# Attention keys turned in blocks of 128, expert numbers cast on VectorE, and a new order for all but the first stage

## The chip, the cores and the metric

The kernel runs on one core of a Trainium2 chip. The metric is the device time of one execution in microseconds. Before the change the median of three runs is 1021.76 us (1020.55 to 1022.34).

## What is computed

Three layers follow one another. Their inputs and outputs are float32.

```python
# 1. local attention: B=4, H=8, S=768, D=64; chunks of 32 queries
for c in range(nc):
    l_start, r_end = max(0, 32*c - 16), min(S, 32*c + 32 + 8)
    k_full = concat([mem_k, k[:, :, l_start:r_end]])        # 8 memory keys + up to 56 keys
    a = softmax(scale * q_c @ k_full.T)                     # with 1e-9 in the sum
    out[:, :, chunk c] = a @ concat([mem_v, v[:, :, l_start:r_end]])
# 2. MLP over 3072 tokens of 512: w_in 512 x 2048, w_out 2048 x 512 (float64 words)
h = x @ w_in;  x = (h * tanh(softplus(h))) @ w_out
# 3. routed MLP: each token goes to one of 8 experts (512 -> 1024 -> 512)
expert_idx = argmax(cosine(x, expert_emb) / tau);  gate = softmax(...)[expert_idx]
out[mask_e] = gate * (relu(x[mask_e] @ w1[e]) @ w2[e])
```

Products that need more than one pass of TensorE's reduced float32 are taken as three: high part by high part, high by low, low by high.

## The kernel before

**Attention.** The work is cut into 24 pairs P, each two blocks of 64 queries; six pairs make one batch. A pair loads its queries (`q`) and its keys in two pieces: `k1`, 8 memory rows and 96 keys (104 rows), and `k2` (72 rows). TensorE turns them (`Tq`, `Tk` 0, `Tk` 1, all on L511) into `p_qT`, `p_kT` and `p_k`. ScalarE or VectorE then copies from these into `kT`, a tile with four groups of 64 columns, one per chunk of 32 queries: 8 memory keys, 24 keys before, 32 of the chunk (three copies from `p_kT`, two from `p_k`, L334). Then come the scores `S` (L559), maximum, exponential, normalization, the transposition `PT` (L602) and the product with the values `V` (L621), whose result is split into `xt`.

**MLP.** Eight blocks of 384 tokens by 16 feature chunks give 128 steps. Step s has `mm_h` (12 matmuls of 384 columns, L732), a chain of about ten element operations on ScalarE and VectorE (L736 to L761), and `mm_y` (9 matmuls of 512 columns, L778). The attention of later blocks runs between the MLP steps of earlier ones.

**Routing and experts.** Tokens are routed in two groups: the first 21 tiles of 128 tokens (group 1) and all (group 2). In a group, VectorE works out positions and counts, TensorE counts (`cnt`, L1060) and builds the table of tokens per slot (`tab`, L1218, copied off by L1230); `ef` holds the expert number of each unit as float32, `ei` the same as integers (L1175). There are 16 units u: 0 to 2 from group 1, the rest from group 2. A unit is a pair of slots (256 tokens) or a single (128). It gathers its tokens (GpSimd, L1288, into `vn`), turns them (`xT`, L1331), splits them (`xs`, L1334 and L1348), loads 8 pieces of expert weights of 512 KB (`eraw`, L1314, address from `ei`, read by L1302; whether it differs from the expert before from `ci`, L1304), splits these in `ehi` (L334) and `elo` (L1367), and multiplies: four `H` (L1395; L1429 for singles) and four to eight `Y` (L1485). The result is scattered by GpSimd (L1511).

**What sets the order.** All steps are jobs of the class `Plan`. `order` is a list scheduler: from the jobs whose predecessors are planned it takes the one of lowest rank among those that can start soonest, with assumed durations (`on=`). The rank is the job's place in the program plus a number from the table `NUDGE`, by kind of job and stage. The outcome is one fixed sequence for each engine, which works through it in order. Waits between engines are semaphores. Loads are issued from SyncE's queue (SP), gathers and scatters from GpSimd's.

Of the kernel before, what the change touches and what calls it, by code (L numbers as in the profile page):

```python
# [86 lines left out]
def between(a, b):  # L87
# [12 lines left out]


NUDGE = dict(
    acta0=-0.6, acta1=-1.74, acta2=50.36, actb0=-1.76, actb1=-96.54, actb2=-81.79, actb3=-42.59, att00=40.88,
    att01=6.03, att02=-14.41, att03=12.63, att04=-3.12, att05=6.33, att06=-6.99, att07=-18.03, att10=10.46, att11=7.93,
    att12=-2.03, att13=-0.28, att14=-5.39, att15=28.34, att16=0.19, att17=-11.65, att20=7.04, att21=-2.49, att22=6.84,
    att23=0.68, att25=11.02, att26=-13.24, att27=2.06, att30=-0.41, att31=-70.31, att32=-0.58, att33=-1.39,
    att35=-0.38, att36=-1.67, att37=-67.52, att40=0.45, att41=-0.43, att42=13.06, att43=-2.17, att44=-38.4,
    att45=12.86, att46=9, att47=-2.37, att50=-1.08, att51=-18.11, att52=-6.46, att53=252.42, att54=-0.22, att55=-3.21,
    att56=-1.09, att57=2.56, att60=-5.29, att61=2.16, att63=-69, att64=-3.49, att65=145.06, att66=-0.33, att67=-14.14,
    att70=-0.37, att71=-329.92, att72=0.25, att73=-193.55, att74=-10.54, att75=-2.18, att76=-1.27, e00=-1.37, e01=8.52,  # L110
    e10=3.1, e11=23.17, e20=-86.99, e21=1, e30=0.07, e31=1.64, e40=10.43, e41=28.57, e50=1.56, e51=-2.1, e60=-22.39,
    e61=17.86, e70=-0.44, e71=-5.41, em=3.37, en0=24.71, en1=-0.52, en2=4.38, en3=27.95, en4=-27.14, en5=-7.94,
    hh0=0.33, hh1=-9.8, hh2=7.9, ld00=-15.25, ld01=24.83, ld10=34.53, ld11=33.12, load0=8.15, load1=17.34, load10=5.31,
    load2=-45.54, load3=-3.15, load4=-2.18, load5=-0.64, load7=3.07, load9=4.58, mm_y0=20.47, mm_y1=14.69, mm_y2=275.2,
    mm_y3=-0.5, out0False=-95.98, out0True=2.61, out1False=4.84, out2False=6.58, raw0=-8.26, raw1=5.15, raw10=24.34,
    raw11=134.61, raw2=-9.44, raw3=-3.37, raw4=-0.07, raw5=-13.38, raw6=29.5, raw7=26.79, raw9=-0.21, route=3.96,
    rows0=21.85, rows1=0.04, rows2=2.04, split0=0.59, split10=130.91, split11=-16.93, split3=-2.85, split4=-6.67,
    split5=17.18, split6=34, split9=27.54, xs0=0.9, xs1=0.33, xs2=-187.61, ye0=0.64, ye1=82.2, ye2=137.26, ye3=-2.03,
    ye4=8.94, ye5=-5.92, yre0=-32.64, yre1=-4.26, yre3=-2.85, yre4=22.58, yre5=-10.72,
)  # L120
ATT = dict(q=0, k1=0, k2=0, Tq=1, Tk=1, qT=1, kT=1, v=2, mem=2, mem0=2, S=3, mx=3, ex=4, rg=5, rc=5, norm=5, PT=6, pT=6, V=7, xh=7, xl=7)

# [42 lines left out]
class Plan:  # L165
# [115 lines left out]
def attn_moe_moe_kernel(ctx, tc, q, k, v, mem_k, mem_v, w_in, w_out, emb, tau, w1, w2, cst, out, ydbg=None):  # L281
# [143 lines left out]
    def pairs(P):  # L425
# [39 lines left out]
        def load_k1(e):  # L465
            if not spare:
                if P == 0:
                    tl["k"] = att.tile([128, H, D], F32, tag="kn", bufs=1, name="kn")
                tl["kn", P] = tl["k"]
            t = tl["kn", P]  # L470
            if spare or i == 0:
                dma(e, t[0:NMEM], mem_k[b].rearrange("h p d -> p h d"))
            get_keys(e, t, NMEM, w, w + K1 - NMEM)

        def load_k2(e):
            t = tl["kn2", P] = wp.tile([K2, H, D], F32, tag=k2t, name="kn2") if first else tl["k"]
# [30 lines left out]
        def turn(name, src, rows):  # L507
            def f(e):
                p, c = psa([128, J, rows], "p_" + name), tl[src, P]
                for n in range(J):  # L510
                    nc.tensor.transpose(p[:, n, :], c[0:rows, 2 * n:2 * n + 2, :].rearrange("p h d -> p (h d)"), ident[:rows, :rows])  # L511
                tl["T", name, P] = p
                if name == "qT":
                    tl["qT", P] = own(qts, [128, J, 2 * QB], "qT", bufs=1)
                if name == "kT":
                    tl["kT", P] = own(ktt, [128, J, 4, SEEN], "kT", bufs=1)
            return f

# [117 lines left out]
        plan.dma(("q", P), load_q, size=rows(128), rank=L(0), after=[("issue", "k2", P - 1)] if P else [], get=[(qkt[0], qs)], **iss(1))  # L639
        plan.dma(("k1", P), load_k1, size=rows(K1), rank=L(0.1), after=[("issue", "q", P)] if P > 1 else [("issue", "k1", 0)] if P else [], get=[] if spare else [("kn", ks)], use=[qs] if spare else [], **iss(3 if i == 0 else 2 if spare else 1, A if P < 2 else "SP"))  # L640
        plan.dma(("k2", P), load_k2, size=rows(K2), rank=L(0.2), after=[("issue", "q" if P < 2 else "k1", P)], get=[(k2t, k2s)], **iss(2 if i == NQB - 2 else 1))
        kh = qs if spare else ks
        vh = [("vn", P, h) for h in range(2)]
        for h in range(2):
# [7 lines left out]
        qh, kt, xb = ("qT", P), ("kT", P), [("X", P, a) for a in range(2)]  # L652
# [275 lines left out]
    def routing():  # L928
# [51 lines left out]
        def group(g):  # L980
# [286 lines left out]
    def unit(u, base, x, cols, main=True, after=0, then=0):  # L1267
# [379 lines left out]
```

## Time and profile before

| | |
|---|---|
| median of 3 runs | 1021.76 us |
| the profiled execution, its own time | 1021.15 us |
| its span, first to last instruction | 1019.4 us |
| mean granted TensorE clock | 0.991 |
| TensorE busy / VectorE busy / ScalarE busy / GpSimd busy | 991.5 / 809.0 / 648.8 / 189.5 us |
| the chain that ended last | TensorE 76%, VectorE 8%, DMA 7%, issue 5% |

The profile is of one execution. TensorE is busy for 97% of the span, in an unbroken stretch from about 110 to 660 us (attention and MLP) and with some gaps behind (routing and experts). The first 110 us load and split the MLP's weights. Row groups below name engines PE (TensorE), DVE (VectorE), ACT (ScalarE), POOL (GpSimd) and SP (SyncE, `SPq` its queue).

### The profile page before, as it was taken

The page shows a single profiled execution, that of the slowest core. Times are in us where ns is not written, and L with a number is a line of the kernel's source. Part 1 is how long each engine was busy: PE and PEld are TensorE (multiplying, and loading weights), DVE is VectorE, ACT ScalarE, POOL GpSimd, SP SyncE. Part 2 cuts the span into 40 slices and gives each one's busy share as a digit, 9 for nine tenths or more (in the row PEclk, how much of TensorE's full clock was granted, in tenths as well). Part 3 has the DMA queues.
Part 4 walks back from the last instruction along what each step waited for, and adds up shares of the span by engine and source line. Part 5 has one row for each costly group of instructions (what it writes and reads, how often), then busy time and mean ns, then how long its engine had stood idle before and what let it go on. Part 6 is the DMA issues. An engine that isn't in the chain of part 4 may idle for free.

```text
span 1019.4 us, 22817 instructions
## 1 busy us (share of the span) xinstructions
PE 991.5 (97%) x8575; PEld 879.2 (86%) x8575; DVE 809.0 (79%) x1799; ACT 648.8 (64%) x1534; POOL 189.5 (19%) x142
## 2 busy tenths in 40 slices
PE   7899999999999999999999999999989999999997
PEld 6678888898888888888888899888979988988986
DVE  4889999669899869769869867979948667777972
ACT  4788888776877777778777767757424334443431
POOL 5000100000000000000000000011136455555742
PEclk9989999999999999999999999999989999999999
DMA  9997661233645234325313100089089868467300
GB/s 181 253 237 200 168 184 45 59 128 97 184 132 135 74 78 134 84 46 145 84 25 122 30 20 20 1 272 327 32 279 371 280 229 296 150 218 246 127 29 23
DMA packets 171817, 146.36 MB, mean 144 GB/s; under 512 B 105114, under 2 KB 134410, under 8 KB 171444
## 3 DMA queue, kind: packets, MB, share of 16 engines
q1 hardware_dynamic: 164868, 128.53, 43.5%
q0 software_dynamic: 5104, 15.89, 4.6%
q8 instruction: 69, 1.13, 0.5%
q10 hardware_dynamic: 1728, 0.43, 0.3%
q14 instruction: 48, 0.39, 0.1%
HBM read 137.11 MB, written 16.53 MB: 151 GB/s over the span
## 4 chain that ended last, share of the span: by engine, by line
PE 76%; DVE 8%; DMA 7%; issue 5%; POOL 2%; SPq 1%; ACT 0%; POOLq 0%; DVEq 0%
PE p_h L732 23%; PE p_y L778 23%; PE p_y L1485 10%; PE p_h L1395 9%; DMA eraw<-in_moe_w_dram 2%; PE p_h L1429 2%; DMA kn<-in_k_dram 2%; PE p_X L621 2%; PE p_S L559 2%; POOL elo L1367 1%; SPq L319 1%; PE p_PT L602 1%; PE p_xT L1331 1%; PE p_qT L511 1%; DMA qn<-in_q_dram 1%
## 5 line engine op out<-in xcount | busy, mean ns | idle before, releaser
L732 PE MATMUL p_h<-xt,win_h 128*128 128x384 f32 x1024 | 268.9, 344 | 0.6 <-DVE rn L761 0.5
L732 PEld LDWEIGHTS p_h<-xt,win_h 128*128 128x128 f32 x1024 | 185.3, 191 | 10.2 <-DVE rn L761 1.8
L732 PE MATMUL p_h<-xt,win_l 128*128 128x384 f32 x512 | 173.9, 340 | 0.0
L334 ACT CAST ehi<-eraw 128x1024 fp32r<-128x1024 f32 x89 | 92.9, 1049 | 120.0 <-PE p_y L1485 67.7
L778 PE MATMUL p_y<-wout_h,gh 128*128 128x512 f32 x384 | 157.1, 409 | 0.0
L778 PE MATMUL p_y<-wout_h,gl 128*128 128x512 f32 x384 | 151.9, 396 | 0.0
L778 PE MATMUL p_y<-wout_l,gh 128*128 128x512 f32 x384 | 151.8, 395 | 0.0
L1367 DVE TENSOR_TENSOR elo<-eraw,ehi 128x1024 fp32r<-128x1024 f32 x89 | 127.9, 1444 | 28.3 <-ACT ehi L334 27.7
L1485 PE MATMUL p_y<-ehi,hh 128*128 128x512 f32 x432 | 144.1, 400 | 0.0
L1395 PE MATMUL p_h<-xs,ehi 128*128 128x256 f32 x704 | 128.3, 283 | 7.0 <-DVE xs L1348 2.5
L755 ACT ACTIVATE m<-m,cf 128x384 f32<-128x384 f32 x128 | 79.1, 618 | 70.6 <-DVE m L751 69.7
L1395 PEld LDWEIGHTS p_h<-xs,ehi 128*128 128x128 f32 x704 | 110.4, 191 | 10.3 <-DVE xs L1348 2.7
L1367 POOL TENSOR_TENSOR elo<-eraw,ehi 128x1024 fp32r<-128x1024 f32 x39 | 94.9, 2432 | 81.1 <-DVE ehi L334 36.6
L851 DVE SCALAR_TENSOR_TENSOR junk<-ysb,en 128x512 f32<-128x512 f32 x144 | 99.0, 688 | 3.0 <-DMA ysb<-y_d 2.7
L1395 PE MATMUL p_h<-xs,elo 128*128 128x256 f32 x352 | 99.3, 282 | 0.0
L732 PEld LDWEIGHTS p_h<-xt,win_l 128*128 128x128 f32 x512 | 97.4, 190 | 0.0
L1485 PEld LDWEIGHTS p_y<-ehi,hh 128*128 128x128 f32 x432 | 80.9, 188 | 18.2 <-DVE hh L1454 0.3
L751 DVE SCALAR_TENSOR_TENSOR m<-sq,rn 128x384 f32<-128x384 f32 x128 | 71.0, 555 | 31.1 <-ACT rn L324 29.8
L758 DVE SCALAR_TENSOR_TENSOR rn<-m,rn 128x384 f32<-128x384 f32 x128 | 71.5, 558 | 30.0 <-ACT m L755 27.9
L736 ACT ACTIVATE sq<-p_h 128x384 f32<-128x384 f32 x128 | 62.8, 491 | 41.2 <-PE p_h L732 40.8
L778 PEld LDWEIGHTS p_y<-wout_h,gl 128*128 128x128 f32 x384 | 72.2, 188 | 17.3
L1485 PE MATMUL p_y<-elo,hh 128*128 128x512 f32 x216 | 85.2, 394 | 0.0
(264 smaller groups left out, 1770.8 us busy)
## 6 DMA issues: line engine op xcount, KB each, us to landing
eraw<-in_moe_w_dram SPq DMA_DIRECT2D x128, 512.0 KB
en<-en_d SPq DMA_DIRECT2D x48, 256.0 KB
vn<-in_v_dram SPq DMA_DIRECT2D x162, 56.0 KB
raw<-in_moe_w_in_dram SPq DMA_DIRECT2D x16, 512.0 KB
raw<-in_moe_w_out_dram SPq DMA_DIRECT2D x16, 512.0 KB
y_d<-ysb SPq DMA_DIRECT2D x24, 256.0 KB
qn<-in_q_dram SPq DMA_DIRECT2D x22, 256.0 KB
ysb<-y_d SPq DMA_DIRECT2D x18, 256.0 KB
```

The lines of the kernel that those rows point to most:

```text
L334: (nc.scalar.copy if e == A else nc.vector.tensor_copy)(out, src)
L559: nc.tensor.matmul(ps[s][r:r + CHUNK, h, n // 2, :], a[64 * s:64 * s + 64, n, QB * h + CHUNK * x:QB * h + CHUNK * x + CHUNK], c[64 * s:64 ...
L732: nc.tensor.matmul(p, w, xt[j][:, a, kk, :], start=(n == 0), stop=(n == len(ops) - 1))
L736: nc.scalar.activation(t, tl["h", s], AF.Tanh, scale=0.5)
L751: nc.vector.scalar_tensor_tensor(t, tl["sq", s], 4.0, tl["rn", s], ALU.add, ALU.mult)
L755: nc.scalar.activation(t, t, AF.Square, bias=c15)
L758: nc.vector.scalar_tensor_tensor(tl["rn", s], tl["m", s], 0.75, tl["rn", s], ALU.add, ALU.mult)
L778: nc.tensor.matmul(yp[yh][t], x[:, c], w[g][:, o, :], start=(first and n == 0), stop=(final and n == 2))
L851: nc.vector.scalar_tensor_tensor(junk, tl["yio", t][:, 1], 1.0, tl["en", j, x], ALU.mult, ALU.mult, accum_out=lg[:, i, x:x + 1])
L1367: engs[e].tensor_sub(tl["elo", j], raw[b, second, c], tl["ehi", j].bitcast(F32))
L1395: nc.tensor.matmul(p[:, o, :], w[:, kk, s], v[:, kk, :], start=(kk == 0 and m == 0), stop=(kk == KDM - 1 and m == 2))
L1485: nc.tensor.matmul(tl["yy", u][a], v[:, kk, s], w[:, k, :], start=(kk == 0 and m == 0), stop=(kk == KEF - 1 and m == 2))
```

## The change

Three parts of code and a table of numbers.

1. `CARRY = 12`: from the 13th pair on (P at least 12, two of the four batches), a pair loads 128 keys once (`k1`) and turns them once. The tile `kT` is kept from pair to pair: `keep` moves the last 24 keys of the fourth group to the front of the first, `fresh_keys` copies the new keys from `p_kT` in two copies. At a batch's first pair (P = 12 and 18) an extra load and transposition of 32 rows (8 memory, 24 keys) fills the start.
2. `numbers`: the cast `ef` to `ei` runs on VectorE as soon as the numbers are worked out, not on GpSimd behind the group's first two gathers.
3. The weight loads of a unit are issued when all of the unit before have been, and the first of them is planned with a longer time on SP.
4. `NUDGE` has other numbers for the stages behind the first.

```diff
+CARRY = 12
...
-    acta0=-0.6, acta1=-1.74, acta2=50.36, actb0=-1.76, actb1=-96.54, actb2=-81.79, actb3=-42.59, att00=40.88,
...
+    acta0=-0.6, acta1=-1.74, acta2=130.07, acta3=-141.75, actb0=-1.76, actb1=-96.54, actb2=102.25, actb3=-232.18,
...
+        carry, start = P >= CARRY, P >= CARRY and i == 0
+        KB = NMEM + PREV
...
 def load_k1(e):
+            if carry:
+                get_keys(e, t, 0, w + PREV, w + PREV + 2 * QB)
+                return
...
+        def keep(e):
+            if P == CARRY:
+                tl["kTs"] = own(ktt, [128, J, 4, SEEN], "kT", bufs=1)
+            t = tl["kT", P] = tl["kTs"]
+            if i == 0:
+                p = tl["T", "k2", P]
+                copy(e, t[:, :, 0, 0:KB], p)
+                x = p[:, :, 0:NMEM]
+                copy(e, t[:, :, 1:4, 0:NMEM], bass.AP(...))
+            else:
+                copy(e, t[:, :, 0, NMEM:KB], t[:, :, 3, SEEN - PREV:])
+
+        def fresh_keys(e):
+            t, p = tl["kT", P], tl["T", "kT", P]
+            copy(e, t[:, :, :, KB:], p.rearrange("p j (c n) -> p j c n", c=4))
+            x = p[:, :, CHUNK - PREV:CHUNK]
+            copy(e, t[:, :, 1:4, NMEM:KB], bass.AP(...))
...
+            job(("Tk", P, 0), turn("kT", "kn", 128), {E: 436}, rank=R(0), after=[("k1", P), ("S", P - 1)], use=[kh], get=[("a", t2)])
...
+            job(("kT", P, 1), keep, ..., after=[("S", P - 1)] + ([("Tk", P, 1)] if start else [("kT", P - 1, 0)]), ...)
+            job(("kT", P, 0), fresh_keys, {A: 830, V_: 1000}, rank=R(1), after=[("Tk", P, 0), ("kT", P, 1), ("S", P - 1)], use=[t2, kt])
...
-                nc.gpsimd.tensor_copy(ei[:, c], ef[:, c])
-            job(("experts", g), numbers, {G: 200}, rank=rk, after=[ex] + [("issue", "gather", first, a) for a in range(2)])
+                nc.vector.tensor_copy(ei[:, c], ef[:, c])
+            job(("experts", g), numbers, {V_: 80}, rank=rk, after=[ex])
...
+                if u and c == 0 and second == 0:
+                    after.append(("issue", "ld", u - 1, 1, NC_ - 1))
```

How the sequences move. In the whole program the plans are the same up to TensorE's step `mm_y` 14, some 148 us into the span. Three places behind it follow.

GpSimd, where routing ends and the expert units begin, before (`vn<-y_d,gi` gathers a unit's tokens, `ei` is the cast, `out_dram` a scatter):

```order
L594 TENSOR_TENSOR pr<-pr,sm 128x256 x5
L1288 DMA vn<-y_d,gi 128x512 x2
L1175 CAST ei<-ef 1x3
L1288 DMA vn<-y_d,gi 128x512 x4
L1511 DMA out_dram<-yo,si 3072x512 x4
L1288 DMA vn<-y_d,gi 128x512 x2
L1175 CAST ei<-ef 1x20
L1367 TENSOR_TENSOR elo<-eraw,ehi 128x1024
```

VectorE at the same place after the change, with the cast of group 2 (`p_tab` is the table of the group, `gi` the gather's addresses):

```order
L1251 TENSOR_TENSOR rhs_9632<-rhs_9632,ra 128x3x32
L1210 CAST ra<-ra 1x3
L1251 TENSOR_TENSOR rhs_9634<-rhs_9634,ra 128x3x32
L1273 COPY ra<-p_tab 128x96
L1218 CAST ei<-ef 1x20
L1251 TENSOR_TENSOR rhs_9636<-rhs_9636,ra 128x3x32
L1274 SCALAR_TENSOR_TENSOR ra<-ra 128x32
L1412 TENSOR_TENSOR elo<-eraw,ehi 128x1024
L1275 CAST gi<-ra 128x32
```

The cast of the 20 numbers stands ahead of the addresses `gi` that the gathers need, where it stood behind the gathers.

SyncE's queue, loads of units 3 and 4, before (`ei` and `ci` are read into registers at a unit's first load; one piece of `eraw` per DMA row):

```order
L1302 TENSOR_LOAD ei
L1302 ISA x2
L1304 TENSOR_LOAD ci
L1304 ISA x2
L1314 ISA
L1314 DMA eraw<-in_moe_w_dram 128x4x256
L1302 TENSOR_LOAD ei
L1302 ISA x2
L1304 TENSOR_LOAD ci
L1304 ISA x2
L1314 ISA
L1314 DMA eraw<-in_moe_w_dram 128x4x256
```

And after, from unit 3's first load on:

```order
L1345 TENSOR_LOAD ei
L1345 ISA x2
L1347 TENSOR_LOAD ci
L1347 ISA x2
L1357 ISA
L1357 DMA eraw<-in_moe_w_dram 128x4x256
L1357 ISA
L1357 DMA eraw<-in_moe_w_dram 128x4x256
L1357 ISA
L1357 DMA eraw<-in_moe_w_dram 128x4x256
L1357 ISA
L1357 DMA eraw<-in_moe_w_dram 128x4x256
```

Before, unit 4's first piece was issued right behind unit 3's first, and the two units took turns; after, unit 3's eight pieces go first.

TensorE, up to the scores of a pair in the second half of the attention, before (`p_k` is the second transposition of the keys):

```order
L732 MATMUL p_h<-xt,win_l 128x384
L511 MATMUL p_k_4276<-cf,kn 128x72 x4
L778 MATMUL p_y_3879<-wout_h,gh 128x512
L778 MATMUL p_y_3879<-wout_l,gh 128x512
L778 MATMUL p_y_3879<-wout_h,gl 128x512
L778 MATMUL p_y_3880<-wout_h,gh 128x512
L778 MATMUL p_y_3880<-wout_l,gh 128x512
L778 MATMUL p_y_3880<-wout_h,gl 128x512
L778 MATMUL p_y_3881<-wout_h,gh 128x512
L778 MATMUL p_y_3881<-wout_l,gh 128x512
L778 MATMUL p_y_3881<-wout_h,gl 128x512
L559 MATMUL p_S<-kT,qT 32x64 x32
```

And after, up to the scores of the 14th pair:

```order
L649 MATMUL p_X<-pT,vn 64x32 x32
L521 MATMUL p_kT<-cf,kn 128x128 x4
L821 MATMUL p_y_3889<-wout_h,gh 128x512
L821 MATMUL p_y_3889<-wout_l,gh 128x512
L821 MATMUL p_y_3889<-wout_h,gl 128x512
L821 MATMUL p_y_3890<-wout_h,gh 128x512
L821 MATMUL p_y_3890<-wout_l,gh 128x512
L821 MATMUL p_y_3890<-wout_h,gl 128x512
L821 MATMUL p_y_3891<-wout_h,gh 128x512
L821 MATMUL p_y_3891<-wout_l,gh 128x512
L821 MATMUL p_y_3891<-wout_h,gl 128x512
L587 MATMUL p_S<-kT,qT 32x64 x32
```

One `mm_y` stands between the last transposition and the scores in both; what is turned there is the whole 128 keys now, where it was the second piece of 72.

## Rows read from the trace of the kernel before

**Rows 1.** Stretches: us, PE, PEld, DVE, ACT, POOL busy (count), clock, DMA share, GB/s.

```profile
120.00:660.00 540.00, 539.72 (x4720) 478.27 (x4718) 446.35 (x1146) 408.62 (x1044) 11.11 (x16) 1.00 0.32 88
...
700.00:740.00 40.00, 40.00 (x286) 36.07 (x285) 38.14 (x142) 21.79 (x31) 8.61 (x7) 1.00 0.32 118
...
760.00:780.00 20.00, 19.56 (x121) 18.40 (x122) 16.26 (x17) 7.43 (x9) 9.67 (x5) 0.86 1.06 376
```

**Rows 2.** Waits of TensorE: us in total, times, longest us.

```profile
PE p_h L1395 <- DVE xs L1348: 2.5, 1, 2.5
PE p_h L1395 <- ACT xs L334: 1.9, 1, 1.9
PE p_h L1395 <- DVE rn L761: 1.8, 1, 1.8
PE p_PT L602 <- DVE kT L334: 1.4, 1, 1.4
...
PE p_h L1395 <- DVE hh L1412: 0.7, 1, 0.7
...
PE p_h L732 <- DVE rn L761: 0.5, 2, 0.3
...
PE p_xT L1331 <- DMA vn<-y_d,gi: 0.3, 1, 0.3
```

**Rows 3.** The chain of waits about unit 3: start us, us, what.

```profile
734.11 0.07 DVE ra L1167
...
734.22 0.25 DVE ra L1230
...
737.38 2.67 POOL vn L1288
...
740.36 1.81 POOL vn L1288
742.17 0.19 POOL ei L1175
...
743.83 3.40 DMA eraw<-in_moe_w_dram
...
749.92 9.15 DMA eraw<-in_moe_w_dram
759.10 0.69 DVE ehi L334
759.79 0.61 DVE xs L1348
...
760.44 13.77 PE p_h L1395 x95
```

**Rows 4.** GpSimd's timeline, group 1: start us, us, line, operation.

```profile
666.59 0.58 POOL L1175 CAST ei<-ef 1x3 int32<-1x3 f32 x1
```

**Rows 5.** TensorE's timeline about two pairs' transpositions, the same columns.

```profile
341.54 0.60 PE L511 MATMUL p_qT<-cf,qn 128*128 128x128 f32 x4
341.90 0.59 PE L732 MATMUL p_h<-xt,win_h 128*128 128x384 f32 x2
...
344.06 0.52 PE L511 MATMUL p_kT<-cf,kn 104*128 104x104 f32 x4
344.36 0.48 PE L778 MATMUL p_y<-wout_h,gh 128*128 128x512 f32 x1
...
348.64 0.41 PE L511 MATMUL p_k<-cf,kn 72*128 72x72 f32 x4
348.85 0.48 PE L778 MATMUL p_y<-wout_h,gh 128*128 128x512 f32 x1
```

**Rows 6.** Copies into `kT`, 250 to 560 us: min/median/max ns, starts, shapes.

```profile
L334 ACT COPY kT<-p_kT x33: 278/337/524, 288.4 to 525.1; 128x384 f32<-128x384 f32 x11, 128x192 f32<-128x192 f32 x11, 128x128 f32<-128x128 f32 x11
```

**Rows 7.** The chain of waits, one `mm_y`: start us, us, what.

```profile
665.85 2.10 PE p_y L778 x9
```

**Rows 8.** The stretch about the longest gap of the attention (columns of rows 1).

```profile
108.00:122.00 14.00, 12.64 (x162) 11.28 (x154) 12.36 (x31) 11.69 (x37) 2.59 (x2) 0.88 0.53 143
```

**Rows 9.** The keys' transpositions, 250 to 560 us (columns of rows 6).

```profile
L511 PE MATMUL p_kT<-cf,kn x48: 250/252/308, 260.2 to 524.0; 104*128 104x104 f32 x48
```

More of the change, by code (lines that the diff above doesn't have):

```diff
@@ L108 @@
[L108 to L117, printed above, removed]
@@ L514, in f @@
                     tl["qT", P] = own(qts, [128, J, 2 * QB], "qT", bufs=1)
-                if name == "kT":
+                if name == "kT" and not carry:
                     tl["kT", P] = own(ktt, [128, J, 4, SEEN], "kT", bufs=1)
@@ L638, in pairs @@
         qs, ks, k2s = ("qn", P), ("kn", P), ("kn2", P)
-        plan.dma(("q", P), load_q, size=rows(128), rank=L(0), after=[("issue", "k2", P - 1)] if P else [], get=[(qkt[0], qs)], **iss(1))
-        plan.dma(("k1", P), load_k1, size=rows(K1), rank=L(0.1), after=[("issue", "q", P)] if P > 1 else [("issue", "k1", 0)] if P else [], get=[] if spare else [("kn", ks)], use=[qs] if spare else [], **iss(3 if i == 0 else 2 if spare else 1, A if P < 2 else "SP"))
-        plan.dma(("k2", P), load_k2, size=rows(K2), rank=L(0.2), after=[("issue", "q" if P < 2 else "k1", P)], get=[(k2t, k2s)], **iss(2 if i == NQB - 2 else 1))
+        plan.dma(("q", P), load_q, size=rows(128), rank=L(0), after=([("issue", "k1" if P > CARRY else "k2", P - 1)] if P else []), get=[(qkt[0], qs)], **iss(1))
+        if not carry:
+            plan.dma(("k1", P), load_k1, size=rows(K1), rank=L(0.1), after=[("issue", "q", P)] if P > 1 else [("issue", "k1", 0)] if P else [], get=[] if spare else [("kn", ks)], use=[qs] if spare else [], **iss(3 if i == 0 else 2 if spare else 1, A if P < 2 else "SP"))
+            plan.dma(("k2", P), load_k2, size=rows(K2), rank=L(0.2), after=[("issue", "q" if P < 2 else "k1", P)], get=[(k2t, k2s)], **iss(2 if i == NQB - 2 else 1))
+        else:
+            if start:
+                plan.dma(("k2", P), load_k2, size=rows(KB), rank=L(0.05), after=[("issue", "q", P)], get=[(k2t, k2s)], **iss(2))
+            plan.dma(("k1", P), load_k1, size=rows(128), rank=L(0.1), after=[("issue", "k2" if start else "q", P)], get=[("kn", ks)], **iss(2 if i == NQB - 2 else 1))
         kh = qs if spare else ks
@@ L651, in pairs @@
         mxh, sm = (pr, pr) if spare else (("mx", P), ("sm", P))
-        qh, kt, xb = ("qT", P), ("kT", P), [("X", P, a) for a in range(2)]
+        qh, kt, xb = ("qT", P), ("kT", min(P, CARRY)), [("X", P, a) for a in range(2)]
         mems = spare or i == 0
@@ L658, in pairs @@
         job(("Tq", P), turn("qT", "qn", 128), {E: 436}, rank=R(0), after=[("q", P)], use=[qs], get=[("a", t1), (qts, qh)])
-        job(("Tk", P, 0), turn("kT", "kn", K1), {E: 350}, rank=R(0), after=[("k1", P)], use=[kh], get=[("a", t2), (ktt, kt)])
-        job(("Tk", P, 1), turn("k2", "kn2", K2), {E: 250}, rank=R(0), after=[("k2", P)], use=[k2s], get=[("a", t3)])
-        job(("qT", P), qT, {A: 478, V_: 598}, rank=R(1), after=[("Tq", P)], use=[t1, qh])
-        job(("kT", P, 0), kT(0), {A: 750, V_: 900}, rank=R(1), after=[("Tk", P, 0)], use=[t2, kt])
-        job(("kT", P, 1), kT(1), {A: 430, V_: 530}, rank=R(1), after=[("Tk", P, 1)], use=[t3, kt])
+        if not carry:
+            job(("Tk", P, 0), turn("kT", "kn", K1), {E: 350}, rank=R(0), after=[("k1", P)], use=[kh], get=[("a", t2), (ktt, kt)])
+            job(("Tk", P, 1), turn("k2", "kn2", K2), {E: 250}, rank=R(0), after=[("k2", P)], use=[k2s], get=[("a", t3)])
+        else:
+            if start:
+                job(("Tk", P, 1), turn("k2", "kn2", KB), {E: 290}, rank=R(0), after=[("k2", P), ("S", P - 1)], use=[k2s], get=[("a", t3)])
+            job(("Tk", P, 0), turn("kT", "kn", 128), {E: 436}, rank=R(0), after=[("k1", P), ("S", P - 1)], use=[kh], get=[("a", t2)])
+        job(("qT", P), qT, {A: 478, V_: 598}, rank=R(1), after=[("Tq", P)], use=[t1, qh])
+        if not carry:
+            job(("kT", P, 0), kT(0), {A: 750, V_: 900}, rank=R(1), after=[("Tk", P, 0)], use=[t2, kt])
+            job(("kT", P, 1), kT(1), {A: 430, V_: 530}, rank=R(1), after=[("Tk", P, 1)], use=[t3, kt])
+        else:
+            job(("kT", P, 1), keep, {A: 420, V_: 400} if start else {A: 160, V_: 115, G: 250}, rank=R(1), after=[("S", P - 1)] + ([("Tk", P, 1)] if start else [("kT", P - 1, 0)]),
+                get=[(ktt, kt)] if P == CARRY else [], use=([t3] if start else []) + ([] if P == CARRY else [kt]))
+            job(("kT", P, 0), fresh_keys, {A: 830, V_: 1000}, rank=R(1), after=[("Tk", P, 0), ("kT", P, 1), ("S", P - 1)], use=[t2, kt])
         job(("S", P), S_, {E: 1000 if edge else 590}, rank=R(1), after=[("qT", P), ("kT", P, 0), ("kT", P, 1)] + prev("S") + ([("ex", 0, 1)] if P == 2 else []) + ([("V", P - 2)] if j > LEAVE and P > SPB // 2 * (LEAVE + 1) else []), use=[qh, kt] + (pss if spare else []),
@@ L1320, in unit @@
                 after = [("experts", g)] + ([("slo", u - 2, second, c)] if u >= 2 else [])
+                if u and c == 0 and second == 0:
+                    after.append(("issue", "ld", u - 1, 1, NC_ - 1))
                 if c or second:
                     after.append(("issue", "ld", u, second, c - 1) if c else ("issue", "ld", u, 0, NC_ - 1))
-                put_job(("ld", u, second, c), load(second, c), dict(SP=470), base - 7 + 1.5 * second + 0.3 * c, after,
+                put_job(("ld", u, second, c), load(second, c), dict(SP=470 + (0 if c or second else 950 if u < 2 else 1450)), base - 7 + 1.5 * second + 0.3 * c, after,
                         [(f"w{8 * b + 4 * second + c}", h)] if u < 2 else [], [] if u < 2 else [h], dma=2 ** 19)
```

28 lines of the change are left out of this document (22 added, 6 removed).

## The prediction

> **What bounds the kernel now.** I read the stretches first, since a share over the whole span mixes stages. From 120 to 660 us TensorE is busy for 539.72 of 540 us at the full granted clock (2.4 GHz) [rows 1]: in attention and MLP the time is TensorE's own work, and only fewer or cheaper instructions there can shorten it. Behind 660 us time is lost in gaps. The waits of TensorE name them [rows 2]: 1.8 us in the first expert unit, 1.9 and 2.5 us in front of unit 3, 0.7 and 0.3 us in two later units. The 1.4 us wait of `p_PT` lies in the first stage, whose order is kept. So the change can win in two places: what it takes off TensorE before 660 us, and which gaps behind it go. Against that stand new gaps.
>
> The chain of waits about unit 3 shows how its gap comes about [rows 3]. The experts' numbers are worked out at 734.18 us (the end of `ra` L1167). The cast that makes integers of them stands on GpSimd behind the two gathers, which begin at 737.38, since they need the slot table (copied at 734.22) and addresses made from it; it runs at 742.17. SyncE reads the numbers then, and the first weights start at 743.83. The fourth piece of unit 3, sharing the engines with unit 4's pieces, starts at 749.92 and needs 9.15 us. The split `ehi` on VectorE waits for it, the tokens' split `xs` stands behind `ehi` in VectorE's queue, and the first matmul of the unit waits for `xs`. The 95 matmuls that follow need 13.77 us. In the window 760 to 780 the mean granted clock is 0.86 [rows 1], part of it at the lower level (1.2 GHz), after the two gaps: 0.14 of 20 us is 2.8 us lost beside the gaps.
>
> **The change part by part.**
>
> Keys in blocks of 128. Start to next start, the four transpositions of 104 rows take 0.30 us, those of 72 rows 0.21, those of 128 rows (the queries') 0.36 [rows 5]. Before, twelve pairs pay 0.51 each, 6.1 us. After, they pay 0.36 each, 4.3 us, and two pairs add one of 32 rows. No row has that size: it lies between 0 and 0.21, and the line from 128 to 72 rows, 0.0027 us a row, gives 0.10, which I take: 0.2 us for two. Gain: 6.1 less 4.3 less 0.2 = 1.6 us, all on TensorE. Ten interruptions of the MLP's stream fall away besides; their price is not in these rows, so I leave it at nothing, with 0.08 us each at most (the spread of 0.30 and 0.35 us is of that size), 0.8 us for the range.
>
> By the Trainium skill ("TensorE: Matmul & The Clock Gate", Part 4: PE-mode transpose) a transposition takes about 275 ns in a kernel, most of it access latency. The single transposition's 252 ns [rows 9] is near that, but the four and the next matmul's start fit in 300 ns [rows 5], so they overlap and the latency is not paid four times. The result that it would give is among the rivals.
>
> The copies into `kT`. `fresh_keys` makes two copies, of 512 and 288 columns a partition. ScalarE's copies from `p_kT` go from 278 ns (128 columns) to 524 (384) [rows 6], 0.96 ns a column, so 0.65 and 0.43, 1.1 us, where three copies of 1.1 us and two of `p_k` stood. ScalarE and VectorE are busy for 409 and 446 of 540 us [rows 1], so less copying gains nothing by itself. The dependency is sharper: `kT` is now one tile, so the old tail moves (`keep`), and new keys come in, only when the scores of the pair before are done. Between the transposition and the scores of the 14th pair stands one `mm_y` of 2.10 us [rows 7] as cover, against 1.1 us of copies and what stands ahead of them on ScalarE (two splits of `p_X`, which two copies of 256 columns by the same line bound at 0.8 us together). That is 1.9 us of 2.1: thin, but it holds. Loads of the keys need not be earlier: one issue less for each of ten pairs frees SyncE and gains nothing, because TensorE waits for no key here.
>
> Cast on VectorE. The instruction itself is a 1 x 20 cast, like `ra` L1167's 0.07 us [rows 3]. It frees the loads from both gathers. At unit 3 the cast follows the table's copy at once: 734.5 instead of 742.36, 7.9 us earlier with nothing else moved. For group 1 the cast at 666.59 [rows 4] stands behind two gathers likewise. The new order also puts the table of group 2 three `Y` steps and the whole of unit 2 ahead of unit 3's first `H`. Behind the table come three `Y`, four `H` and four `Y` before unit 3: eleven steps of 2.8 us (12 matmuls of 512 columns at the 2.10 / 9 of [rows 7]; an `H` has 24 of half the columns), 30.8 us. If VectorE copies the table some 5 us late, as I estimate from its full queue there, unit 3's loads have 25 us; they had 11.7 (from 743.83 to 755.6, which is 760.44 less both waits and one matmul of 0.4). Eight pieces of 512 KB at 376 GB/s [rows 1] take 11.2 us. All of them land in time, whatever their order.
>
> One unit's loads at a time. The fourth piece no longer shares the engines with unit 4's pieces. That alone would bring it forward (four pieces, 2.1 MB, in about 5.6 us at the same rate). Unit 4's pieces come later by that, but its matmuls begin some 24 us behind unit 3's, so they are covered.
>
> So the two gaps before unit 3 go, 1.9 + 2.5, and the half clock behind them, 2.8: 7.2 us. Unit 0's gap of 1.8 us goes with the earlier cast and with routing moved ahead by three to four MLP steps. The gaps of 0.7 and 0.3 us I take as gone too, as the new order draws these stages apart, between 0 and 1.0: 1.0.
>
> Costs. The new order makes its own small gaps. Those of the MLP now are two of 0.3 us at most [rows 2]; two more are 0.6. And `cnt` of group 2 stands nearer to the VectorE steps that it needs, between 0 and 2 us of wait; I take 0.5, because VectorE reaches that place about when TensorE does.
>
> Sum: −1.6 − 7.2 − 1.8 − 1.0 + 0.6 + 0.5 = −10.5. The profiled execution took 1021.15 us, 0.6 below the median of the runs shown. 1021.15 − 10.5 = 1010.65; for the median I add 0.6 back: 1011.2.
>
> **Rivals.**
>
> Unit 3 still waits (0.06). If what gates it is not the weights but the gather or `xs`, the 7.2 us stay: 1018.4. For it: `xs` is the name in the wait. Against: `xs` stood behind an `ehi` that waited for a load. VectorE's queue is first in, first out by the Trainium skill ("TensorE: Matmul & The Clock Gate", the table at its head), and the order on 759.10 and 759.79 [rows 3] agrees; by that rule the new cast, too, can't pass the copy of `p_tab` before it, which only costs the lead named above.
>
> Routing of group 2 holds up TensorE (0.12). The new order has one `Y` step and three turnings of tokens fewer between `cnt` and the table, 2.8 + 3 x 0.36 = 3.9 us less time for VectorE's steps there, and from 700 to 740 VectorE is busy for 38.14 of 40 us [rows 1]. If it comes 2 to 4 us late, the gap and the lower clock behind it (as much again as at unit 3, 2.8) cost 4.8 to 6.8: 1016 to 1018. Against: part of that busy time is the splitting of the weights of units 1 and 2, which may stand behind the routing.
>
> Gaps in the MLP (0.09). Around 110 us one wait of 1.4 us [rows 2] came with a mean clock of 0.88 over 14 us [rows 8], 1.7 us more: 3.0 in all. Three such where scores or `mm_h` come late give 9 us: 1020.
>
> Slower (0.05). The one-tile chain, scores, `keep`, `fresh_keys`, next scores, leaves TensorE waiting at each pair from the 13th on. Its place is the scores behind a single `mm_y`, its price 3.0 us a pair as above, so twelve pairs make 36 us: 1047. It decides from four pairs on (1023), and from five the kernel is slower. Against: 0.2 us of cover are left on the thinnest place even with ScalarE's splits in front, and other pairs have more between.
>
> Latency paid by each transposition (0.01). Were the 252 ns [rows 9] serial and near the same at every size, twelve pairs would save four times 0.25, 12.0 us, and two would pay 2.0 again: 10.0 instead of 1.6 gives 1002.8. It is what the rule of Part 4 would come to. Against: the 0.30 us of four with what follows [rows 5].
>
> **How the numbers follow.** The forecast has 0.67, with its own ends at 1007 (all costs nothing, 0.8 for interruptions, and the 0.6 us of spread between runs) and 1014 (1.0 not won, costs twice as large). The range goes on into the routing rival: 1006.5 to 1016.5. Changes under 0.2%, about 2 us, can't be told from none here. Faster by more: the forecast, the first two rivals, half of the MLP's gaps and the last, 0.90. Within: the other half, 0.05. Slower: 0.05.
>
> **What would show it.** Right: 14 second transpositions of keys instead of 24, no wait at the first `H` of unit 3, a clock of 1.00 from 740 to 780, the cast on VectorE some microseconds after `tab`, unit 3's loads started over 20 us before its first matmul. Wrong: a TensorE wait on `kT` behind 250 us, on `cnt` or `tab`, or a clock under 1.00 between 150 and 660 us.

## The result and the profile after

The changed kernel takes 1008.26 us (median of 4 runs, 1007.53 to 1010.74) against 1021.15 us beside it: a ratio of 0.9878, 95% interval 0.9856 to 0.9900, 12.5 us faster. Forecast were 1011.2 us, in a range of 1006.5 to 1016.5. A second comparison of the same two kernels (a_after below) gave 0.9874 (0.9856 to 0.9892). In the code of after, line numbers are 1 to 45 higher.

Stretches of the changed kernel, columns as in [rows 1]:

```profile
120.00:660.00 540.00, 539.99 (x4733) 479.49 (x4732) 437.21 (x1139) 423.89 (x1063) 10.66 (x13) 1.00 0.34 95
...
700.00:740.00 40.00, 40.00 (x285) 36.47 (x284) 36.93 (x131) 20.30 (x26) 14.72 (x6) 1.00 0.41 146
740.00:760.00 20.00, 20.00 (x135) 17.69 (x134) 11.77 (x15) 7.38 (x10) 8.79 (x6) 1.00 1.07 369
760.00:780.00 20.00, 20.00 (x134) 17.73 (x132) 12.69 (x17) 6.62 (x9) 11.16 (x7) 1.00 0.85 289
```

TensorE is busy throughout from 700 to 780 at the full clock, where it lost 4.4 us to two gaps and worked at 0.86 behind them. Its waits, the list from the fourth line to the eighth (the ninth is 0.2 us at the start), answer to [rows 2]:

```profile
PE p_PT L630 <- DVE kT L335: 1.4, 1, 1.4
PE p_X L649 <- DVE pr L622: 0.6, 1, 0.6
PE p_kT L521 <- DMA qkn<-in_k_dram: 0.6, 1, 0.6
PE p_qT L521 <- DMA qn<-in_q_dram: 0.5, 1, 0.5
PE p_h L775 <- DVE rn L804: 0.3, 1, 0.3
```

No line of the routing or the experts is left in it. The cast and the loads, VectorE's timeline (start us, us) and SyncE's (start us, us over a group of issues):

```profile
721.62 0.24 DVE L1273 COPY ra<-p_tab 128x96 f32<-128x96 f32 x1
721.78 0.15 DVE L1218 CAST ei<-ef 1x20 int32<-1x20 f32 x1
...
723.27 0.16 DVE L1275 CAST gi<-ra 128x32 int32<-128x32 f32 x1
```

```profile
723.41 8.95 SPq L1357 DMA_DIRECT2D eraw<-in_moe_w_dram  x10
```

Unit 3's loads start at 723.4 and its first `H` at 753.7: 30 us of lead, where [rows 3] had 11.8 until TensorE wanted the weights.

One thing is new and costs. TensorE's timeline behind the MLP (start us, us, line, operation, count) and two stretches (columns of rows 1):

```profile
687.89 1.47 PE L882 MATMUL p_yT<-cf,ysb 128*128 128x128 f32 x12
689.21 2.97 PE L903 MATMUL p_lg<-cf,yt 128*128 128x8 f32 x24
692.04 1.18 PE L1376 MATMUL p_xT<-cf,vn 128*128 128x128 f32 x8
692.87 0.78 PE L1530 MATMUL p_y<-ehi,hh 128*128 128x512 f32 x1
```

```profile
688.00:692.00 4.00, 4.00 (x37) 3.86 (x36) 2.32 (x4) 3.73 (x8) 0.00 (x0) 1.00 0.97 248
692.00:696.00 4.00, 4.00 (x17) 3.33 (x17) 2.43 (x10) 3.24 (x6) 1.90 (x2) 0.61 0.32 95
```

For 5 us TensorE does only transpositions and matmuls of 8 columns. It waits for nothing, and behind them the clock goes to its lower level for most of 4 us (0.61): a `Y` takes 4.4 us instead of 2.8. The profiled run took 1010.74 us.

### The profile page after: what moved, and what is told of

The parts are those of the page before. It is cut to its first block, busy times and chain, and to the rows that moved or that the text cites. A ratio compares the mean times of both kernels' runs of the same rounds, so it can differ in the third digit from the quotient of the medians.

```text
span 1009.0 us, 22842 instructions
## 1 busy us (share of the span) xinstructions
PE 987.8 (98%) x8535; PEld 877.5 (87%) x8535; DVE 772.4 (77%) x1762; ACT 665.8 (66%) x1557; POOL 187.5 (19%) x134
## 5 line engine op out<-in xcount | busy, mean ns | idle before, releaser
L1412 DVE TENSOR_TENSOR elo<-eraw,ehi 128x1024 fp32r<-128x1024 f32 x89 | 116.1, 1316 | 23.0 <-ACT ehi L335 21.9
L1440 PE MATMUL p_h<-xs,ehi 128*128 128x256 f32 x704 | 126.0, 280 | 0.0
L622 POOL TENSOR_TENSOR pr<-pr,sm 128x256 f32<-128x256 f32 x12 | 9.4, 787 | 462.3 <-DVE sm L617 139.0
```

The costliest lines, as they stand in the source:

```text
L622: engs[e].tensor_tensor(t, t, r.rearrange("p (a n) -> p a n", n=1).to_broadcast([2 * QB, J, SEEN]), ALU.mult)
L1412: engs[e].tensor_sub(tl["elo", j], raw[b, second, c], tl["ehi", j].bitcast(F32))
L1440: nc.tensor.matmul(p[:, o, :], w[:, kk, s], v[:, kk, :], start=(kk == 0 and m == 0), stop=(kk == KDM - 1 and m == 2))
```

## The experiments

All programs here, e8_gap but for its one edit, are the same up to TensorE's `mm_y` 14. In the profiles that step starts between 141.3 and 149.7 us (144.7 before, 146.0 in the changed kernel), so what comes before scatters by more than the terms in dispute. I therefore read each profile's timeline from there: to the start of `mm_y` 115, of unit 3's first `H`, of unit 5's, and of the last matmul (us). In the kernels with the new order, `mm_y` 115 comes one `mm_h` (2.1 us) later in the sequence, so 2.1 us of the second stretch are in the first. Each row is one profile, while the ratio is of all runs. The first stretch has the same TensorE sequence in before, e1_cast, e2_loads, e3_both, e7_small and e10_group2, and takes 482.6 to 483.5 us there. That of the changed kernel is also the one of a_after, e5_back, e6_apart and e8_gap, and takes 481.9 to 483.4 us. So two profiles that differ by 1 us in it need not differ for any cause.

| kernel | ratio to before (95%) | to `mm_y` 115 | to unit 3 | to unit 5 | to the end | sum |
|---|---|---|---|---|---|---|
| before | | 482.6 | 130.3 | 53.1 | 203.1 | 869.1 |
| changed | 0.9878 (0.9856 to 0.9900) | 482.4 | 125.4 | 47.9 | 201.8 | 857.4 |
| a_after (changed, again) | 0.9874 (0.9856 to 0.9892) | 483.4 | 123.8 | 47.9 | 201.7 | 856.8 |
| e1_cast | 0.9939 (0.9917 to 0.9960) | 483.3 | 129.3 | 47.9 | 203.4 | 863.8 |
| e2_loads | 0.9985 (0.9969 to 1.0000) | 483.5 | 132.2 | 48.7 | 202.2 | 866.6 |
| e3_both | 0.9926 (0.9905 to 0.9948) | 483.4 | 128.5 | 47.9 | 202.5 | 862.2 |
| e10_group2 | 0.9915 (0.9892 to 0.9938) | 482.9 | 131.3 | 47.9 | 202.7 | 864.7 |
| e5_back | 0.9937 (0.9913 to 0.9960) | 482.6 | 134.3 | 47.9 | 202.1 | 866.8 |
| e9_keys | 1.0012 (0.9995 to 1.0029) | 483.1 | 131.6 | 52.1 | 202.8 | 869.6 |
| e4_nocarry | 1.0010 (0.9990 to 1.0029) | 494.7 | 125.3 | 47.9 | 201.7 | 869.6 |
| e6_apart | 0.9882 (0.9865 to 0.9900) | 482.5 | 123.7 | 47.9 | 202.0 | 856.0 |
| e8_gap | 0.9855 (0.9827 to 0.9882) | 481.9 | 123.7 | 47.9 | 201.8 | 855.3 |
| e7_small | 1.0030 (1.0009 to 1.0050) | 483.3 | 136.6 | 53.5 | 202.7 | 876.1 |

**The cast alone (e1_cast).** `move` takes a job of the finished sequence and puts it behind another.

```diff
+        for g in (1, 2):
+            move(("experts", g), self.jobs["experts", g]["after"][0], "DVE")
...
-                nc.gpsimd.tensor_copy(ei[:, c], ef[:, c])
+                nc.vector.tensor_copy(ei[:, c], ef[:, c])
```

> The kernel before, with one edit: both casts of the experts' numbers stand on VectorE, right behind the step that makes the numbers; every other instruction stands where it stood, and the loads of units 3 and 4 still take turns. Theory A (the lead of the loads decides): in the profile of before the cast ran at 742.2 us and the numbers were there at 734.2; unit 3's loads start 7.9 us earlier, the fourth piece lands near 751 instead of 759, ahead of the first H at 755.6, and unit 0's by as much; the waits of 1.9, 2.5 and 1.8 us and the lower clock behind unit 3 go: about 9 us faster (ratio 0.991). Rival B (turn-taking with unit 4's pieces decides): about half of unit 3's wait stays, with the lower clock behind it: 3 to 4 us faster. Rival C (the tokens' gather or split is what is late): no change.

Measured: about 6 us faster, not 9. Unit 3 is as A says: 47.9 instead of 53.1, and no wait. At unit 0 the wait of 1.8 us is gone but another of 3.3 us stands in its place; a line of TensorE's waits and two of the chain (start us, us, what):

```profile
PE p_xT L1340 <- DMA vn<-y_d,gi: 3.6, 2, 3.3
```

```profile
658.27 3.60 DMA eraw<-in_moe_w_dram
661.88 7.41 DMA vn<-y_d,gi
```

Unit 0's weights now start ahead of its gather, which takes 7.4 us. Before, the gather started at 664.2 and TensorE turned its tokens at 668.3 without a wait, so there it took 4.1 us at most. B and C fall.

**Group 2's cast alone (e10_group2).** As above, with `for g in (2,)` and group 1's cast left on GpSimd.

> The kernel before with the cast of group 2 alone on VectorE, right behind the numbers; group 1's cast stays on GpSimd behind unit 0's gathers. With both casts moved (e1_cast) the weights of unit 0 started at 658.3 us, ahead of unit 0's gathers at 661.9 and 663.3, the gather then took 7.4 us and TensorE waited 3.3 us for it. Theory A (the gather is late because the weights load beside it): here unit 0's loads stand behind its gathers again, the wait at xT is 0.3 us or less, the 1.8 us wait of unit 0's second H is back, and unit 3's waits are gone: from step 14's mm_y to the end 7 us less than before, and 1 to 2 us less than e1_cast (ratio to before 0.993). Rival B (the gather was late for a reason of its own): the wait at xT stays.

Measured: unit 0's `xT` doesn't wait (the 0.3 us that is left stands at a later unit, at 831.9 us, as in before), the wait of unit 0's second `H` is back (2.2), unit 3 waits for nothing. So the gather was late because weights were loading beside it. The Trainium skill ("DMA: Bandwidth & Descriptors", Issuing engines are not separate DMA queues) says that transfers from whichever engine run on the same 16 DMA engines and interleave; the 7.4 us agree. The ratio of 0.9915 fits the forecast 0.993, and by the ratios this kernel is 2.5 us faster than e1_cast, on another chip and with overlapping intervals. The sums of the profiles say otherwise, 864.7 against 863.8: the profiled run took 1016.77 us, where the median is 1013.85, and the lower clock behind that gap (0.83 from 680 to 690) and behind the logits (below) came on top in it.

**Loads one unit at a time (e2_loads), and both (e3_both).**

```diff
...
+        at = [n for n, (k, e) in enumerate(seq) if k and k[:2] == ("issue", "ld") and k[2] in (0, 1, 3, 4)]
+        for n, x in zip(at, sorted(seq[n] for n in at)):
+            seq[n] = x
...
```

> The kernel before, with one edit: units 0 and 1, and units 3 and 4, load one after the other instead of in turns; the casts stay on GpSimd behind the gathers. Theory A: the loads still start at 743.8 us, 11.8 ahead of unit 3's first H; its four first pieces, 2.1 MB, need about 6 us when nothing else shares the engines, so they land near 750 and this edit alone also removes the waits at units 0 and 3: 7 to 9 us faster, the two edits being substitutes. Rival B (only the start counts): the waits shrink by less than half, 0 to 3 us faster.

> The kernel before with both edits, cast on VectorE and loads one unit at a time. Theory A: 9 to 10 us faster, no more than the better of the two alone, since each takes the same waits away; what is left to the whole change's 12.5 us (some 3) is the new order in the MLP. Rival B (each removes another part): the gains of the two add up.

Measured: e2_loads gains 1.5 us (its interval ends at no gain), neither A nor B as a whole. At unit 3 it is A: 48.7, with one wait of 0.6 us left, though the loads start no earlier. At unit 0 it makes a new wait. VectorE's timeline there [idle before]:

```profile
678.49 0.68 DVE L1416 SCALAR_TENSOR_TENSOR hh<-p_h,hh 128x512 fp32r<-128x512 f32 x1
685.93 2.36 DVE L1371 TENSOR_TENSOR elo<-eraw,ehi 128x1024 fp32r<-128x1024 f32 x2 [6.75 <-ACT ehi L338]
688.21 0.69 DVE L1416 SCALAR_TENSOR_TENSOR hh<-p_h,hh 128x512 fp32r<-128x512 f32 x1
```

and TensorE's wait for it:

```profile
PE p_h L1399 <- DVE hh L1416: 4.5, 1, 4.5
```

The old order of VectorE and ScalarE has unit 1's splits between unit 0's, as the loads took turns. With unit 1's weights later, VectorE stands for 6.75 us before a split that unit 0 doesn't need (the first of the two at 685.93), and unit 0's own split and `hh`, which TensorE needs, stand behind it. (VectorE's queue is strictly first in, first out by the Trainium skill, "TensorE: Matmul & The Clock Gate", the table at its head; these rows agree.) With both edits, 7.5 us faster. By the times alone B can't be told from A, since the single gains, 6.2 and 1.5, add up to 7.7. The stretches tell them apart: at unit 3 the two are substitutes (47.9 with both and with the cast alone, 48.7 with the loads alone). What e3_both has over e1_cast, 1.6 us of the sum, lies elsewhere: 0.8 before unit 3, where the wait for `hh` doesn't come and the gather's is 2.5 us instead of 3.3, and 0.9 in the last stretch. The gather's wait is most of what is missing to A's 9 to 10.

**The new order with the old cast (e5_back).** The changed kernel, and:

```diff
...
+        for g, u in ((1, 0), (2, 3)):
+            move(("experts", g), ("issue", "gather", u, 1), "Pool")
+            at = [k for k, e in seq if k and k[:3] == ("issue", "ld", u)]
+            n = seq.index((("experts", g), "Pool"))
+            for k in reversed([k for k in at if seq.index((k, "SP")) < n]):
+                move(k, ("experts", g))
...
-                nc.vector.tensor_copy(ei[:, c], ef[:, c])
+                nc.gpsimd.tensor_copy(ei[:, c], ef[:, c])
```

> The changed kernel with one edit: the casts of the experts' numbers are back on GpSimd, behind the group's two gathers, and the weight loads that read them follow; the order of all other work is the new one. In the changed kernel the numbers of group 2 are cast at 721.8 us, the second gather of unit 3 ends on GpSimd near 732, unit 3's first H starts at 753.7. Theory A (the new order carries the lead, the cast is a second remedy for the same wait): unit 3's loads start near 734 and have 20 us left, 11 are needed, so no wait comes back at unit 3; at unit 0 the loads start 6 us later, and ScalarE and VectorE, where the splits stand among the MLP's steps, lose up to 6 us: 0 to 4 us slower than the changed kernel (ratio to before 0.988 to 0.992). Rival B (the cast carries the gain): the waits of before come back, 7 us or more slower than the changed kernel (0.995 or more).

Measured: 6.4 us slower than the changed kernel beside it by the ratios, between A's 0 to 4 and B's 7; the interval reaches into both. Single runs go from 1008.79 to 1018.88 us, and the profiled one took 1018.88. Unit 3 as A says: 47.9, no wait, so even the late cast is covered there: unit 3's loads start at 743.5, 18 us ahead of its first `H`. They also still go one unit at a time, so this isn't the order's doing alone. The loss of the profile is at unit 0 (134.3 against 125.4). ScalarE's timeline and TensorE's waits:

```profile
654.91 1.05 ACT L348 CAST ehi<-eraw 128x1024 fp32r<-128x1024 f32 x1 [6.74 <-DMA eraw<-in_moe_w_dram]
```

```profile
PE p_h L1453 <- DVE rn L817: 2.5, 1, 2.5
...
PE p_h L788 <- DVE rn L817: 1.7, 3, 1.3
...
PE p_y L834 <- DVE gh L348: 0.6, 1, 0.6
```

The new order puts unit 0's splits among the last MLP steps. Weights that start 6 us later (23.9 us behind `mm_y` 115, where the changed kernel has 17.8) stop ScalarE there, and with it the MLP's own chain. TensorE's three waits there are 4.3 us. The lower clock behind the last of them (0.58 from 680 to 684) costs about 1.7 us, and behind the logits it costs about 3.4 here and 1.6 in the changed kernel's profile; the rest of the 8.9, about 1 us, I can't place. So the early cast of group 1 is a condition of the new order.

The new order is a condition of the early cast too, though not by putting the gather first. In the changed kernel unit 0's weights start ahead of its gather, as in e1_cast. SyncE's, GpSimd's and TensorE's timelines:

```profile
646.14 33.33 SPq L1357 DMA_DIRECT2D eraw<-in_moe_w_dram  x23
648.55 1.08 POOL L1331 DMA_INDIRECT vn<-y_d,gi  x1 [73.55 <-DVE si L1278]
658.87 0.60 PE L1376 MATMUL p_xT<-cf,vn 128*128 128x128 f32 x4
```

TensorE turns the tokens 10.3 us behind the gather's start. In e1_cast it wanted them 4.2 us behind it (661.88 to 666.1), so the 7.4 us showed.

**The keys alone (e9_keys), and all but the keys (e4_nocarry).** The first keeps before's sequence and puts the new work in the old places, the second is one number.

```diff
...
+            f["Tk", P, 0]["fn"], f["Tk", P, 1]["fn"] = (turn("k2", "kn2", KB) if start else None), turn("kT", "kn", 128)
+            f["kT", P, 0]["fn"], f["kT", P, 1]["fn"] = keep, fresh_keys
```

```diff
-CARRY = 12
+CARRY = 24
```

> The kernel before with the keys' part of the change alone: the order of before is kept, each 128-row transposition stands where the 72-row one stood, the 104-row one is left out (at the two batch starts the 32-row one stands there), keep stands where the first copies stood and not before the scores of the pair ahead, fresh_keys where the second copies stood. Casts, loads and all else are those of before. Theory A: 12 x (0.30 + 0.22) us of transpositions become 12 x 0.36 to 0.41 and 2 x 0.22 to 0.36, with ten interruptions of the MLP fewer, each worth some 0.07: 1 to 2.5 us faster, and the scores, with 1.1 us of copies behind a 2.1 us step, don't wait. Rival B (the copies into the one tile are late): waits of p_S for kT at several pairs with the lower clock behind them, 3 us or more slower.

> The changed kernel with CARRY = 24, so that no pair keeps its keys: all pairs load and turn 104 and 72 rows as before; the other parts of the change and its table of numbers stay, and the planner lays the attention of the later pairs anew. Theory A: in the changed kernel's trace the keys' transpositions cost 0.7 us less in all than before, and fewer interruptions of the MLP some 1 to 2; without them 1 to 3 us slower than the changed kernel (ratio to before 0.989 to 0.991), if the new plan makes no gap. Rival B (the keys carry the MLP's gain and more): 4 us or more slower than the changed kernel. Rival C (the planner's order falls apart without the numbers found for it): gaps of over 1 us in the MLP, 5 us or more slower.

Measured: e9_keys is not faster (1.0012; 869.6 against 869.1), so neither A nor B. Its transpositions of keys take 6.0 us where before's take 7.2 (from `mm_y` 14 to 115, summed start to next start; one that a wait of 0.4 us follows is counted without it). Of the 1.2 us saved, three small waits for `rn`, 0.9 us in all where before has 0.2, use up part; the rest is inside the scatter of the stretch. e4_nocarry is 12 us slower than the changed kernel by the stretches, all of it before `mm_y` 115: C. Its waits from 250 to 660 us:

```profile
PE p_PT L630 <- DVE pr L622: 2.1, 2, 1.2
PE p_X L649 <- ACT pT L335: 1.3, 2, 0.7
PE p_kT L521 <- DMA kn<-in_k_dram: 1.2, 1, 1.2
```

With them came a clock of 0.53 from 368 to 379. Read by itself, this run would give the keys 12 us. It shows only that the planner, with the keys' part taken out, makes another order, one with gaps; that this is because the numbers were found for a program with that part is my reading. What the keys are worth within the new order is open.

**The run of small matmuls (e6_apart, e7_small).**

```diff
...
+        chain = [("r", 86), ("Y", 0, 1), ("xT", 1, 0), ("issue", "gather", 2, 0), ("xT", 1, 1), ...]
+        move(("Y", 0, 0), ("yb1", 22))
+        for ref, key in zip(chain, chain[1:]):
+            move(key, ref)
...
```

```diff
...
+        for ref, key in ((("yL2", 21), ("xT", 1, 0)), (("yL2", 22), ("xT", 1, 1)), (("xT", 1, 1), ("Y", 0, 0)), (("Y", 0, 0), ("Y", 0, 1))):
+            move(key, ref)
...
```

> The changed kernel with its order edited at one place: between the transpositions of the last three token tiles and their logits stands a step Y of unit 0, and a second one between the logits and the transpositions of unit 1's tokens. In the changed kernel these stand in one run from 687.9 to 692.9 us (12 transpositions, 24 matmuls of 8 columns, 8 transpositions), TensorE waits for nothing there, and still the granted clock falls to 0.61 in the 4 us behind it; the next Y takes 4.4 us instead of 2.8. Theory A (the run of small matmuls brings the clock down): the clock stays at 1.00 from 680 to 700, and the kernel is 1.6 to 2.3 us faster than the changed one (ratio to before 0.986). Rival B (the clock falls there for another reason, for instance with the load that follows): no change.

> The kernel before with one edit to TensorE's order: unit 0's first two Y steps stand behind the logits of the last three token tiles and the transpositions of unit 1's tokens, so that 12 transpositions, 24 matmuls of 8 columns and 8 transpositions follow one another as in the changed kernel, where the clock fell behind them in one profile (0.61 from 692 to 696) and not in another. Theory A (such a run can bring the clock down): a granted clock under 0.9 in the 4 us behind the run, 1.5 to 2.5 us lost there, in this profile or not in every one. Rival B (the new order's other neighbours were the reason): the clock stays at 1.00 behind it.

> The changed kernel itself, for a comparison on one chip with the kernels beside it: 0.988 of before.

Measured: e6_apart's clock stays at 1.00 there, and its time is that of the changed kernel (1007.51 and 1007.41 us on one chip): A's gain doesn't show. The second profile of the changed kernel (a_after) shows why one profile can't decide. The clock does not fall in it, and its stretch to unit 3 is 123.8, 1.6 less than in the first profile and the same as e6_apart's 123.7. The fall comes in some executions only. e7_small is inconclusive: waits of 1.0 and 1.8 us came into the run, so the 0.50 behind it is not that of a run without waits. But e10_group2, in before's order and without a wait there, shows it: TensorE's timeline, and the stretch behind:

```profile
696.87 0.60 PE L848 MATMUL p_yT<-cf,ysb 128*128 128x128 f32 x4
697.30 2.75 PE L869 MATMUL p_lg<-cf,yt 128*128 128x8 f32 x24
699.91 0.48 PE L1494 MATMUL p_y<-ehi,hh 128*128 128x512 f32 x1
```

```profile
702.00:706.00 4.00, 4.00 (x18) 2.93 (x17) 1.46 (x6) 1.72 (x4) 0.00 (x0) 0.66 1.06 388
```

So it isn't the new order's own, either.

Two runs made for other ends have the new order's run of small matmuls too, whole and without a wait in it. The stretch behind it, in e5_back, e4_nocarry, a_after and e6_apart (columns of rows 1):

```profile
698.00:704.00 6.00, 6.00 (x22) 5.23 (x22) 2.82 (x10) 3.31 (x7) 1.90 (x2) 0.50 0.32 90
702.00:706.00 4.00, 4.00 (x16) 3.28 (x15) 2.03 (x8) 3.18 (x6) 1.90 (x2) 0.60 0.32 85
696.00:700.00 4.00, 4.00 (x27) 3.54 (x27) 3.08 (x10) 3.10 (x7) 1.90 (x2) 1.00 0.37 116
692.00:696.00 4.00, 4.00 (x24) 3.42 (x24) 1.67 (x8) 0.12 (x1) 0.00 (x0) 1.00 0.01 4
```

With the run whole the clock falls in three profiles of four, with the run broken up in neither of two (e6_apart, e8_gap); behind before's shorter run without waits in one of six. That speaks for A, but it is few profiles: that the small matmuls bring the clock down is not shown, and a gain from breaking them up isn't either.

**A gap of the first stage (e8_gap).** e6_apart, and:

```diff
...
+        move(("kT", 8, 1), ("Tk", 8, 1))
+        move(("lo", 17), ("m", 9), "Pool")
...
```

> The kernel e6_apart with one more edit, in the first stage that before and after have in common: VectorE's copy of the keys of pair 8 (kT 8, second piece) stands right behind their transposition, ahead of two other steps, and the low part of weight piece 17 is made on GpSimd. In all profiles so far TensorE waits 1.1 to 1.4 us there for that copy (p_PT <- DVE kT). Theory A: the wait shrinks to 0.7 or less and with it the lower clock behind it where there is one: 0.7 to 2.5 us faster than e6_apart (ratio 0.985 to 0.987). Rival B (VectorE is full there, busy for 19.7 of 20 us, so the wait only moves to another instruction): no change.

Measured: the wait shrinks to 0.7 us, with one of 0.3 behind it; 1007.09 us, ratio 0.9855. Its interval overlaps those of the changed kernel and of e6_apart, so a gain over them isn't shown. It has the lowest ratio of all that ran; its sum in the table leaves the edited place out.

## Why the prediction was right

The direction, the size and the range held. Step by step, with the sum of the changed kernel's profile from `mm_y` 14 on, 869.1 less 857.4 = 11.7 us:

- Unit 3, 7.2 forecast: right. The stretch from unit 3 to unit 5 lost 5.2, and the `Y` step before it 2.15 with its gap: 7.4. But that the cast "frees the loads from both gathers" is one of several sufficient causes: one unit's loads at a time does nearly the same (e2_loads), and the two other parts together do it without the early cast (e5_back). The order alone was not run. The prediction listed all three and priced them once, which is what saved the sum.
- Unit 0, 1.8 forecast: right in size (2.2, what is left of the stretch to unit 3 when the other terms are taken off), and right that it "goes with the earlier cast and with routing moved ahead". It needs both, for a reason that the prediction doesn't have: the earlier cast alone turns it into a 3.3 us wait for the gather (e1_cast), the rest of the change without it into waits of the MLP (e5_back). The step priced what was removed and didn't ask what the earlier loads collide with.
- Small gaps of later units, 1.0 forecast: 1.4 in the last stretch. Other kernels in before's order have 202.2 to 203.4 there, those in the new one 201.7 to 202.1, so 0.1 to 1.7.
- Keys, 1.6 forecast: mis-sized. The transpositions save 0.7 in the changed kernel (7.2 to 6.5). Nine of its twelve transpositions of 128 rows stand behind other small matmuls (the scores, the product with `V`), and there four of them take 0.41 us to the next start and not 0.36:

```profile
265.29 0.43 PE L521 MATMUL p_k<-cf,kn 32*128 32x32 f32 x4
265.65 0.51 PE L821 MATMUL p_y<-wout_h,gh 128*128 128x512 f32 x1
...
283.61 0.66 PE L521 MATMUL p_kT<-cf,kn 128*128 128x128 f32 x4
284.02 0.48 PE L821 MATMUL p_y<-wout_h,gh 128*128 128x512 f32 x1
```

 The one of 32 rows takes 0.36 to the next start, in e9_keys behind the MLP's matmuls too, above the bound of 0.21 that the prediction set for it from the 72 rows. The copies cost what was forecast (0.69 and 0.45 us on VectorE at the most, on ScalarE 0.60 and 0.40), and the slower rival (scores waiting at each pair) didn't come.
- Costs of the new order, 0.6 forecast as a loss: this step failed in its sign. The first stretch gains 2.3 (482.6 to 482.4 with one `mm_h` of 2.1 more in it; 1.3 in a_after). On average the five profiles of the new sequence, without that `mm_h`, are 2.7 below the six of the old. 0.7 of it are the keys' transpositions above, about 1.6 to 2 the order's. Most of that lies in `mm_y`: its 909 matmuls of the stretch take, summed start to next start, 218.3 us before and 218.9 in e9_keys, which has the keys but not the order, and 216.2 in the changed kernel and 216.5 in e4_nocarry, which has a new order without the keys. Which part of the order does it no run shows.
- `cnt`, 0.5 forecast: no wait. In its place the clock behind the logits, 1.6 us in this execution.

With these, 7.4 + 2.2 + 1.4 + 0.7 + 1.6 − 1.6 = 11.7. That the forecast of 10.5 comes near is luck in part: the keys were put 0.9 too high, the order's cost 2.2 the wrong way, and a fall of the clock that the prediction doesn't have took 1.6 back. The two large terms, unit 3 and unit 0, are right on their own.

The rival on the routing (VectorE late at the table) didn't come: the numbers were ready at 721.8 us, though VectorE was busy for 36.9 of 40 us.

## What to carry to other kernels

An early transfer is not free: ask which later one it now runs beside, and whether anything in order queues behind its arrival. Two remedies of one wait are to be priced once, each alone may open another wait. A part taken out of a searched order and planned anew measures the search, not the part: keep the sequence and edit it.

## What was not expected of the hardware

TensorE's granted clock fell to 0.61 and 0.66 over 4 us behind 24 matmuls of 8 columns and transpositions without any idle time among them, in one of two profiles of the changed kernel (and in e4_nocarry and e5_back) and in one of a kernel in before's order, whose own profile doesn't have it. Whether these matmuls are the cause is open. Four transpositions cost more right behind small matmuls (0.41 us against 0.36), and four of 32 rows no less than four of 128 (0.36). An indirect gather of 128 rows took 7.4 us beside weight loads, where 4.1 us were enough without them.
